# Moving six GEMM blocks of batch 0 into the attention of batch 1, with q,k transposed earlier and v loaded later

## Chip, cores and metric

The kernel runs on one core of a Trainium2 chip. The metric is the device time in microseconds (us) of one execution; before the change it is 345.62 us, the median of 3 runs (345.62 to 345.96).

Engines are named as in the profile: PE is TensorE's matmul, PEld its weight load, DVE is VectorE, ACT is ScalarE, POOL is GpSimd, SP is SyncE (which only issues transfers here). A name such as L375 is line 375 of the kernel.

## What is computed

Eight batches of an attention with forget gates, each with 8 heads, 576 positions and 64 elements a head, and after it a two-layer network with exact Gelu over the 4608 resulting rows.

```python
# attention: q, k, v are (8, 8, 576, 64) float32, f is (8, 8, 576)
scores = scale * np.matmul(q, k.transpose(0, 1, 3, 2))
cum = np.cumsum(np.log(np.clip(f, 0.0001, 1.0)), axis=-1)
decay = cum[:, :, :, None] - cum[:, :, None, :]
scores = np.where(causal, -1e9, scores + decay)
attn = softmax(scores)                 # max taken off, exp, divided by the sum
out = np.matmul(attn, v)
# network: w_in is (512, 2048), w_out (2048, 512)
x = out.transpose(0, 2, 1, 3).reshape(4608, 512)
h = x @ w_in
g = 0.5 * h * (1.0 + erf(h / sqrt(2)))
return g @ w_out
```

## The kernel before

All of it works in bfloat16 with float32 sums. Heads are taken in pairs (`i` = 0 to 3). For one pair the scores stand transposed, keys on partitions, in four tiles (`t` = 0 to 3); ACT takes the exp; POOL masks the diagonal blocks (in batch 0, and for the first pair of batch 1, PE adds the mask instead). The decay is not added to the scores: v is weighed with a factor for each key (`weigh_v`, on POOL), and a further column holds the weights themselves, so that the AV product gives sum and normalizer together. DVE normalizes, and PE transposes x again for the first GEMM.

The first GEMM of a batch is 16 blocks of 128 columns of w_in (`ffb` = 0 to 15), each four matmuls of 128x512 and a Gelu on ACT. The second GEMM of a batch is spread between the scores of the next batch's attention (`take(fill, n)` takes n of its matmuls). That can't be done with all of batch 0's second GEMM in batch 1, where only its first half for two row blocks (`gemm2_half(0, 0)`, 16 matmuls) is taken; the rest goes into batch 2.

PSUM has eight banks: two score tiles of two banks (`s`), two `o` banks and two `m` banks.

```python
s_psum = ctx.enter_context(tc.tile_pool(name="s_psum", bufs=2, space=PSUM))
o_psum = ctx.enter_context(tc.tile_pool(name="o_psum", bufs=2, space=PSUM))
m_psum = ctx.enter_context(tc.tile_pool(name="m_psum", bufs=2, space=PSUM))
...
v_sb = consts.tile([P, H, NBLK, D], FP32)          # one buffer for v of any batch
...
def transposes_first(b, i, which, pool, tag):      # q or k of a head pair, 12 transposes
    src = qk_of[b][which]
    ps = pool.tile([P, JT, PT], BF16, tag=tag, name="ps_f")
    ...
    op = nc.scalar.copy if b == i == which == 0 else nc.vector.tensor_copy
    op((qT, kT)[which][i]..., ps...)
...
def weigh_v(b, i, eng=nc.gpsimd):
    ...
    eng.tensor_tensor(vw_of[b][:, hs, :, 0:D], v_sb[:, hs, :, :], w..., Alu.mult)
    eng.tensor_copy(vw_of[b][:, hs, :, D], w)
...
def gemm1(c, ffb, kts=range(4), ps=None, act=True):
    src = xT(c) if c < B else tails
    if ps is None:
        ps = m_psum.tile([P, TC], FP32, tag="m", name="ps1")
    for kt in kts:
        nc.tensor.matmul(ps, w_in_sb[:, kt, ffb * P : (ffb + 1) * P], src[:, kt, 0:TC],
                         start=(kt == 0), stop=(kt == n_dm - 1))
    if n_dm - 1 in kts and act:
        gelu(c, ffb, ps)
    return ps
```

In the attention of batch 0 the loads for what follows are issued (q, k and w by POOL, v by SP):

```python
load_w_in(0)
weigh_v(0, 1)
load_w_in(1)
weigh_v(0, 2)
weigh_v(0, 3)
nc.gpsimd.memset(v_sb[:, :, 0, 0:1], 0.0)
load_v(1, 0, 4)
load_v(1, 4, 8)
load_w_in(2)
load_w_in(3)
load_qk_tokens(1, 0, 4)
load_qk_tokens(1, 4, 8)
```

The attention of batch 1, and the loop around it:

```python
FILL_1 = [[0, 0, 0, 0], [0, 0, 0, 0], [2, 2, 2, 2], [2, 2, 2, 2]]
...
def second_attention():
    b, fill = 1, gemm2_half(0, 0)
    ...
    nc.scalar.activation(warm[0:1, 0:1], warm[0:1, 0:1], Act.Exp)   # loads the exp table
    weigh_v(1, 2)
    weigh_v(1, 3)
    for i in range(HP):
        for t in range(4):
            scores(b, i, t)
            if i == 0 and t < 3:
                transposes(t + 1, *((m_psum, "m") if t == 1 else (o_psum, "o")))
            take(fill, FILL_1[i][t])
            if i and t in (1, 2):
                av(i - 1, t - 1)
            if i > 1 and t == 0:
                to_xT(b, i - 2, nc.vector.tensor_copy, o_psum, "o")
            if (i, t) == (1, 3):
                load_qk_tokens(2, which="k")
            if (i, t) == (3, 0):
                transpose_dma(2, 0, 4)
                transpose_dma(2, 4, 8)
    to_xT(b, HP - 2, nc.vector.tensor_copy, o_psum, "o")
    av(HP - 1, 0)
    av(HP - 1, 1)
    both = s_psum.tile([P, 2, 1024], BF16, tag="s", name="ps_x2")
    gemm1_begin(1, both)          # blocks 0 to 3 of the first GEMM, around the last x transposes
    x_tail(1)
    load_w_out(2)
    load_w_out(3)
    load_v(2)

for b in range(B):
    ...                            # the attention of batch b; batch 0 does blocks 0 to 3 too
    for ffb in range(0 if b > 1 else 4, n_ff):
        gemm1(b, ffb)
        if b == 0:
            if ffb == 14:
                for which in range(2):
                    transposes_first(1, 0, which, o_psum, "o")
            if ffb == 12:
                weigh_v(1, 0)
                load_w_out(0)
                load_w_out(1)
                weigh_v(1, 1)
                load_qk_tokens(2, which="q")
        elif b + 1 < B:
            first, gap = (5, 3) if b == 1 else (0, 4)
            at, late = divmod(ffb - first, gap)
            if late == 0:
                untangle(b + 1, at)        # DVE: q,k of the next batch in their order
            if late == gap - 2:
                weigh_v(b + 1, at)
            ...
```

Of the kernel before, what the change touches and what calls it, by code (L numbers as in the profile page):

```python
# [8 lines left out]
FP32 = mybir.dt.float32  # L9
BF16 = mybir.dt.bfloat16  # L10
Act = mybir.ActivationFunctionType
# [7 lines left out]
HP = 4  # L19
# [33 lines left out]
def kernel(  # L53
# [60 lines left out]
    def load_v(b, h0=0, h1=H):  # L114
        if b >= B:
            return
        for n in range(NBLK):
            p0 = D if n == NBLK - 1 else 0
            nc.sync.dma_start(
                v_sb[p0:P, h0:h1, n, :],  # L120
                v[b, h0:h1, K0[n] + p0 : K0[n] + P].rearrange("h p d -> p h d"),
            )
# [48 lines left out]
    def load_w_out(c):  # L171
        kt = slice(c * n_ff // 4, (c + 1) * n_ff // 4)
        nc.gpsimd.dma_start(w_out_sb[:, kt, :], w_out_r[:, kt, :])
# [5 lines left out]
    cum = consts.tile([BH, S], FP32)  # L179
    wk = f_sb  # L180
    warm = consts.tile([P, TC], BF16)
    nc.vector.memset(warm, 0.0)
    nc.vector.memset(ones, 1.0)
    nc.vector.memset(wT[0:D, 4, :], 0.0)
# [68 lines left out]
    def weigh_v(b, i, eng=nc.gpsimd):  # L253

        if b not in vw_of:
            vw_of[b] = v_pool.tile([P, H, NBLK, D + 1], BF16, tag="vw", name=f"vw{b}")
        hs = slice(2 * i, 2 * i + 2)
        bh = b * H + 2 * i
        w = wT[:, :, bh : bh + 2].rearrange("p n h -> p h n")
        eng.tensor_tensor(  # L260
            vw_of[b][:, hs, :, 0:D],
            v_sb[:, hs, :, :],
            w.unsqueeze(3).to_broadcast([P, 2, NBLK, D]),
            Alu.mult,
        )
        eng.tensor_copy(vw_of[b][:, hs, :, D], w)
# [79 lines left out]
    def to_xT(b, i, copy, pool=m_psum, tag="m", ps=None):  # L346
        if ps is None:
            shape = [P, 2, 1024] if pool is s_psum else [P, XC]
            ps = pool.tile(shape, BF16, tag=tag, name="ps_x")
            if pool is s_psum:  # L350
                ps = ps[:, 0, 0:XC]
        for m in range(NBLK):
            nc.tensor.transpose(  # L353
                ps[:, m * P : (m + 1) * P], x_of[b, i][:, m, :, :], ident_bf
            )
        copy(xT(b)[:, i, :], ps)  # L356
# [10 lines left out]

    g_of = {}

    def gemm1(c, ffb, kts=range(4), ps=None, act=True):  # L370
        src = xT(c) if c < B else tails
        if ps is None:
            ps = m_psum.tile([P, TC], FP32, tag="m", name="ps1")
        for kt in kts:
            nc.tensor.matmul(  # L375
                ps,
                w_in_sb[:, kt, ffb * P : (ffb + 1) * P],
                src[:, kt, 0:TC],
                start=(kt == 0),
                stop=(kt == n_dm - 1),  # L380
            )
        if n_dm - 1 in kts and act:
            gelu(c, ffb, ps)
        return ps

    def gelu(c, ffb, ps):
        if c not in g_of:
# [133 lines left out]
    def take(gen, n):  # L521
        for _ in range(n):
            if next(gen, "end") == "end":
                return


    def first_attention():


        def transposes(i, pool, tag):  # L530
            transposes_first(0, i, 0, pool, tag)
            transposes_first(0, i, 1, pool, tag)

        def attend_head(i, h):
            attend(0, i, h, (0, 1, 2, 3, 4))
            normalize(0, i, h)

        warm_up(11)
        transposes(0, o_psum, "o")
        nc.vector.tensor_copy(key_of[D:P], key_of[0:D])  # L540
        nc.vector.tensor_copy(after[D:P], after[0:D])
        warm_up(2)
        scores(0, 0, 0)
        scores(0, 0, 1)
        transposes(1, m_psum, "m")
        scores(0, 0, 2)
        psw = o_psum.tile([P, NBLK, BH], FP32, tag="o", name="psw")
        for n in range(NBLK):
            nc.tensor.transpose(
                psw[:, n, :], wk[:, K0[n] : K0[n] + P], ident_fp[:BH, :BH]  # L550
            )
        scores(0, 0, 3)
        nc.vector.tensor_copy(wT[:, 0:4, :], psw[:, 0:4, :])
        nc.vector.tensor_copy(wT[D:P, 4, :], psw[D:P, 4, :])
        scores(0, 1, 0)
        transposes(2, m_psum, "m")
        scores(0, 1, 1)
        scores(0, 1, 2)
        transposes(3, m_psum, "m")
        scores(0, 1, 3)  # L560
        weigh_v(0, 0, nc.vector)
        gate = x_pool.tile([P, 1], FP32, tag="gate", name="gate")
        nc.gpsimd.tensor_copy(gate[D:P], v_sb[D:P, 0, 4, 0:1])
        load_w_in(0)
        weigh_v(0, 1)
        load_w_in(1)
        weigh_v(0, 2)
        weigh_v(0, 3)
        nc.gpsimd.memset(v_sb[:, :, 0, 0:1], 0.0)
        load_v(1, 0, 4)  # L570
        load_v(1, 4, 8)
        load_w_in(2)
        load_w_in(3)
        load_qk_tokens(1, 0, 4)
        load_qk_tokens(1, 4, 8)
        scores(0, 2, 0)
        scores(0, 2, 1)
        scores(0, 2, 2)
        scores(0, 2, 3)
        attend_head(0, 0)  # L580
        scores(0, 3, 0)
        attend_head(0, 1)
        scores(0, 3, 1)
        attend_head(1, 0)
        scores(0, 3, 2)
        attend_head(1, 1)
        scores(0, 3, 3)
        to_xT(0, 0, nc.vector.tensor_copy)
        attend_head(2, 0)
        attend_head(2, 1)  # L590
        to_xT(0, 1, nc.scalar.copy)
        attend_head(3, 0)
        both = s_psum.tile([P, 2, 1024], BF16, tag="s", name="ps_x2")
        to_xT(0, 2, nc.scalar.copy, ps=both[:, 0, 0:XC])
        attend_head(3, 1)
        gemm1_begin(0, both)
# [19 lines left out]

    FILL = [[7, 6, 3, 3], [1, 3, 3, 2], [1, 3, 3, 3], [1, 3, 3, 3], [8]]
    FILL_2 = [[8, 8, 8, 8], [8, 8, 4, 4], [4, 4, 4, 4], [4, 4, 4, 4], [8]]
    FILL_1 = [[0, 0, 0, 0], [0, 0, 0, 0], [2, 2, 2, 2], [2, 2, 2, 2]]

    def attention(b):

# [33 lines left out]
    def second_attention():  # L656


        b, fill = 1, gemm2_half(0, 0)

        def av(i, h):
            attend(b, i, h, (0, 1, 2, 3, 4))
            normalize(b, i, h)

        def transposes(i, pool, tag):
            for which in range(2):
                transposes_first(b, i, which, pool, tag)


        nc.scalar.activation(warm[0:1, 0:1], warm[0:1, 0:1], Act.Exp)  # L670
        weigh_v(1, 2)
        weigh_v(1, 3)
        for i in range(HP):
            for t in range(4):
                scores(b, i, t)
                if i == 0 and t < 3:
                    transposes(t + 1, *((m_psum, "m") if t == 1 else (o_psum, "o")))
                take(fill, FILL_1[i][t])
                if i and t in (1, 2):
                    av(i - 1, t - 1)  # L680
                if i > 1 and t == 0:
                    to_xT(b, i - 2, nc.vector.tensor_copy, o_psum, "o")
                if (i, t) == (1, 3):
                    load_qk_tokens(2, which="k")
                if (i, t) == (3, 0):
                    transpose_dma(2, 0, 4)
                    transpose_dma(2, 4, 8)
        to_xT(b, HP - 2, nc.vector.tensor_copy, o_psum, "o")
        av(HP - 1, 0)
        av(HP - 1, 1)  # L690
        both = s_psum.tile([P, 2, 1024], BF16, tag="s", name="ps_x2")
        gemm1_begin(1, both)
# [7 lines that stand above are left out]
            first_attention()  # L700
        elif b == 1:
            second_attention()
        else:
            attention(b)
        if b == 0:
            x_tail(0)
        for ffb in range(0 if b > 1 else 4, n_ff):
            gemm1(b, ffb)
            if b == 0:
                if ffb == 14:  # L710
                    for which in range(2):
                        transposes_first(1, 0, which, o_psum, "o")
                if ffb == 12:
                    weigh_v(1, 0)
                    load_w_out(0)
                    load_w_out(1)
                    weigh_v(1, 1)
                    load_qk_tokens(2, which="q")
            elif b + 1 < B:
                first, gap = (5, 3) if b == 1 else (0, 4)  # L720
                at, late = divmod(ffb - first, gap)
                if late == 0:
                    untangle(b + 1, at)
                if late == gap - 2:
                    weigh_v(b + 1, at)
                if ffb == (9 if b == 1 else 14):
                    load_qk_tokens(b + 2)
# [34 lines left out]
```

The softmax here doesn't subtract the row's maximum and nothing guards it: scores larger than these inputs give would overflow.

## Time and profile before

| | |
|---|---|
| time, median of 3 runs | 345.62 us |
| span of the profiled execution | 343.4 us |
| TensorE clock granted | 0.999 |
| DMA packets, bytes, mean rate | 99924, 43.03 MB, 125 GB/s |
| ACT, all Gelus (L392) | 144 of 597 ns |
| ACT, all exps (L299) | 128 of 836 ns on average |
| POOL, one weighing of v for a head pair (L260) | 1278 ns |
| POOL, one mask (L301) | 383 ns on average |

The profile is of one execution, with times from the span's start. A chain is followed back from the last instruction: at each step to what released it. A line of the chain gives start, length, engine, the tile written and the line. A line of the timeline adds shapes, and in brackets the idle time before it and what ended that. In a row of windows each engine has its busy us in the stretch and in brackets the number of its instructions. Matmuls overlap, so that a matmul's listed duration is longer than what it adds.

### The profile page before, as it was taken

The numbers are of one execution on the slowest core, as the hardware profiler recorded it, in microseconds if no ns is written. First come the engines' busy times: TensorE is split into PE (matmuls) and PEld (weight loads), VectorE is DVE, ScalarE is ACT, GpSimd is POOL, SyncE is SP. The second block draws the span as 40 slices with busy tenths as digits, with TensorE's granted clock in tenths as the row PEclk, the third lists the DMA queues.
The fourth block names the chain that finished last, engine by engine and source line by source line (L and its number), as shares of the span: only waits on it lengthen the run. The fifth ranks groups of instructions, "written<-read, shape, count | busy, mean of one in ns | idle before, by whom it ended". The sixth has DMA issues, their size and how long they took to land.

```text
span 343.4 us, 7895 instructions
## 1 busy us (share of the span) xinstructions
PE 328.6 (96%) x3182; PEld 174.7 (51%) x3227; DVE 187.0 (54%) x424; ACT 212.3 (62%) x296; POOL 124.2 (36%) x256
## 2 busy tenths in 40 slices
PE   7799999999999999999999999999999999999995
PEld 3574555445554456545654565446544654444443
DVE  5660355933467935796479646974597542020011
ACT  5986786773644787368746874687468755504600
POOL 8390672228328034543445243714261430000000
PEclk9999999999999999999999999999999999999999
DMA  8999999989993999578945896499900230011013
GB/s 117 178 176 194 201 166 153 170 158 148 237 184 102 139 192 188 82 101 165 211 121 73 141 212 139 71 160 198 169 31 2 65 88 31 2 61 61 0 38 87
DMA packets 99924, 43.03 MB, mean 125 GB/s; under 512 B 78704, under 2 KB 95344, under 8 KB 99888
## 3 DMA queue, kind: packets, MB, share of 16 engines
q1 hardware_dynamic: 82592, 28.37, 41.4%
q0 software_dynamic: 16896, 13.63, 27.2%
q8 instruction: 25, 0.41, 0.5%
q10 hardware_dynamic: 400, 0.52, 0.4%
q14 instruction: 11, 0.09, 0.1%
HBM read 36.85 MB, written 9.44 MB: 135 GB/s over the span
## 4 chain that ended last, share of the span: by engine, by line
PE 89%; issue 2%; POOL 2%; DVE 2%; ACT 2%; DMA 2%; POOLq 0%; ACTq 0%; DVEq 0%
PE ps L375 36%; PE ps L466 25%; PE o L320 9%; PE ps L408 8%; PE s L289 7%; PE ps L501 2%; ACT e L299 2%; DMA k<-in_k_dram 2%; PE ps_x L353 1%; DVE x L334 1%; POOL q L107 1%; PE ps_f L206 1%; POOL k L107 1%; DVE r L333 0%; DVE xT L356 0%
## 5 line engine op out<-in xcount | busy, mean ns | idle before, releaser
L392 ACT ACTIVATE g<-ps 128x512 bf16<-128x512 f32 x144 | 85.3, 597 | 81.1 <-PE ps L375 81.1
L299 ACT ACTIVATE e<-s 128x896 bf16<-128x896 f32 (+2 forms) x128 | 101.2, 836 | 28.5 <-PE s L289 26.8
L375 PE MATMUL ps<-xT,w_in_sb 128*128 128x512 bf16 x497 | 111.4, 379 | 0.8
L466 PE MATMUL ps<-w_out_sb,g 64*128 64x512 bf16 (+1 forms) x731 | 103.0, 376 | 0.8 <-issue 0.8
L375 PEld LDWEIGHTS <-w_in_sb 128*128 128x128 bf16 x576 | 56.0, 98 | 67.5 <-issue 1.8
L301 POOL TENSOR_SCALAR_AFFINE_SELECT e<-e 128x256 bf16<-128x256 bf16 (+1 forms) x135 | 49.2, 383 | 98.9 <-ACT e L299 98.6
L466 PEld LDWEIGHTS <-g 64*128 64x128 bf16 (+1 forms) x756 | 41.5, 94 | 40.4 <-issue 11.9
L244 DVE COPY qT<-tq 64x288 bf16<-64x288 bf16 x96 | 48.7, 507 | 1.4
L289 PE MATMUL s<-qT,kT 64*128 64x320 bf16 (+4 forms) x384 | 45.8, 276 | 3.6 <-ACT e L299 2.7
L260 POOL TENSOR_TENSOR vw<-v_sb,wT 128x640 bf16<-128x640 f32 x31 | 39.6, 1278 | 23.5 <-DMA v_sb<-in_v_dram 23.3
L320 PE MATMUL o<-vw,e 128*128 128x65 bf16 x960 | 36.8, 194 | 3.5 <-issue 2.4
L474 DVE COPY ot<-ps 128x512 f32<-128x512 f32 x26 | 17.9, 689 | 37.1 <-PE ps L466 35.2
L320 PEld LDWEIGHTS <-e 128*128 128x128 bf16 x960 | 34.8, 98 | 5.3 <-PE ps_x L353 0.3
L244 DVE COPY kT<-tk 64x288 bf16<-64x288 bf16 x96 | 33.0, 343 | 1.6
L334 DVE TENSOR_TENSOR x<-o,r 128x320 bf16<-128x320 f32 x64 | 31.4, 491 | 2.4 <-DVE r L333 0.2
L417 DVE COPY ot<-ps 128x512 f32<-128x512 f32 (+2 forms) x9 | 5.7, 632 | 48.8 <-PE ps L408 31.9
L289 PEld LDWEIGHTS <-kT 64*128 64x128 bf16 x384 | 19.5, 94 | 23.2 <-issue 9.7
L408 PE MATMUL ps<-w_out_sb,g 128*128 128x512 bf16 (+2 forms) x142 | 27.9, 355 | 0.1
L333 DVE RECIPROCAL r<-o 128x5 f32<-128x5 f32 x64 | 12.1, 189 | 27.6 <-PE o L320 27.5
L408 PEld LDWEIGHTS <-g 128*128 128x128 bf16 x144 | 13.5, 98 | 14.5
L476 DVE TENSOR_TENSOR ot<-ot,ps 128x512 f32<-128x512 f32 x26 | 17.9, 687 | 1.5
L365 POOL COPY tails<-xT 128x256 bf16<-128x256 bf16 x8 | 3.2, 399 | 31.3 <-DVE xT L356 31.3
(64 smaller groups left out, 158.1 us busy)
## 6 DMA issues: line engine op xcount, KB each, us to landing
out_dram<-ot SPq DMA_DIRECT2D x32, 256.0 KB, 2.3
v_sb<-in_v_dram SPq DMA_DIRECT2D x24, 256.0 KB, 5.3
q<-in_q_dram POOLq DMA_DIRECT2D x6, 576.0 KB, 6.1
k<-in_k_dram POOLq DMA_DIRECT2D x6, 576.0 KB, 8.2
v_sb<-in_v_dram SPq DMA_DIRECT2D x22, 128.0 KB, 5.1
w_in_sb<-in_moe_w_in_dram POOLq DMA_DIRECT2D x4, 512.0 KB, 6.7
w_out_sb<-in_moe_w_out_dram POOLq DMA_DIRECT2D x4, 512.0 KB, 8.4
q<-in_q_dram POOLq DMA_DIRECT2D x4, 144.0 KB, 4.6
```

What stands on the lines that cost most here:

```text
L244: nc.vector.tensor_copy(rows[:, odd], src[odd * D : (odd + 1) * D, 2 * i + h].rearrange("d j p -> d p j"),)
L260: eng.tensor_tensor(vw_of[b][:, hs, :, 0:D], v_sb[:, hs, :, :], w.unsqueeze(3).to_broadcast([P, 2, NBLK, D]), Alu.mult,)
L289: nc.tensor.matmul(to, *ab, start=half < 0, stop=half == 1 or not masked)
L299: nc.scalar.activation(et[:, :, z:c], st[:, :, z:c], Act.Exp, scale=scale)
L301: nc.gpsimd.affine_select(out=et[:, :, c0 + z : c0 + P], in_=et[:, :, c0 + z : c0 + P], compare_op=Alu.is_ge, fill=0.0, base=z, pattern=[[ ...
L320: nc.tensor.matmul(o[:, m, :], e_of[b, i, t][:, h, c : c + P], vw_of[b][:, 2 * i + h, n, :], start=(n == 0), stop=(n == m),)
L334: nc.vector.tensor_tensor(x_of[b, i][:, :, h, :], o[:, :, 0:D], r.unsqueeze(2).to_broadcast([P, NBLK, D]), Alu.mult,)
L375: nc.tensor.matmul(ps, w_in_sb[:, kt, ffb * P : (ffb + 1) * P], src[:, kt, 0:TC], start=(kt == 0), stop=(kt == n_dm - 1),)
L392: nc.scalar.activation(g_of[c][ffb], ps, Act.Gelu)
L408: nc.tensor.matmul(pss[ts][:, c0:c1], g_of[c][kt][:, ts * P : (ts + 1) * P], w_out_sb[:, kt, c0:c1], start=(kt == 0), stop=(kt == n_ff - 1),)
L466: nc.tensor.matmul(banks[r], g_of[c][kt][rows, ts * P : (ts + 1) * P], w_out_sb[rows, kt, :], start=kt == (steps.index("r") if r else 0), ...
L474: nc.vector.tensor_copy(ot, banks[1])
```

## The change

Six of the sixteen blocks (10 to 15) of batch 0's first GEMM are taken out of their place ahead of batch 1's attention and are computed between its scores. Their result is copied by DVE to SBUF (`h`), and their Gelu is taken later, in batch 1's first GEMM, so that ACT need not change its table between exps. That GEMM's odd blocks take an `o` bank, so that it has four banks.

Along with that: q and k of batch 1 are transposed a pair ahead, the first pair between blocks 8 and 9; scores are issued two at a time; AV products follow from the fifth group of scores on; v of batch 1 is loaded after w_in has landed (a small POOL copy waits for that), not beside the q and k loads; w_out, the weighing of v and the q,k loads of batch 2 are issued later. The purpose is that PE has other work where it waited for DVE's copies and ACT's exps, and that what is needed first is loaded first.

```diff
@@ -179,6 +179,8 @@
     warm = consts.tile([P, TC], BF16)
+    put_off = range(10, 16)
+    h_of = {n: consts.tile([P, TC], FP32, name=f"h{n}") for n in put_off}
@@ -367,10 +369,10 @@
-    def gemm1(c, ffb, kts=range(4), ps=None, act=True):
+    def gemm1(c, ffb, kts=range(4), ps=None, act=True, pool=m_psum, tag="m"):
         src = xT(c) if c < B else tails
         if ps is None:
-            ps = m_psum.tile([P, TC], FP32, tag="m", name="ps1")
+            ps = pool.tile([P, TC], FP32, tag=tag, name="ps1")
@@ -382,6 +384,16 @@
+    def gemm1_late(c):
+
+        for ffb in put_off:
+            ps = m_psum.tile([P, TC], FP32, tag="m", name="ps1")
+            for kt in range(n_dm):
+                gemm1(c, ffb, (kt,), ps, False)
+                if kt == n_dm - 1:
+                    nc.vector.tensor_copy(h_of[ffb], ps)
+                yield
@@ -566,9 +578,6 @@
         weigh_v(0, 3)
-        nc.gpsimd.memset(v_sb[:, :, 0, 0:1], 0.0)
-        load_v(1, 0, 4)
-        load_v(1, 4, 8)
         load_w_in(2)
@@ -616,7 +625,6 @@
-    FILL_1 = [[0, 0, 0, 0], [0, 0, 0, 0], [2, 2, 2, 2], [2, 2, 2, 2]]
@@ -666,26 +674,38 @@
+        transposes(1, m_psum, "m")
         nc.scalar.activation(warm[0:1, 0:1], warm[0:1, 0:1], Act.Exp)
-        weigh_v(1, 2)
-        weigh_v(1, 3)
-        ... (the loop over i and t above)
-        to_xT(b, HP - 2, nc.vector.tensor_copy, o_psum, "o")
+        wide = gemm1_late(0)
+
+        def x_first(i):
+            to_xT(b, i, nc.vector.tensor_copy, o_psum, "o")
+
+        between = [
+            lambda: take(wide, 8),
+            lambda: take(wide, 6),
+            lambda: (transposes(2, o_psum, "o"), take(wide, 2)),
+            lambda: (transposes(3, o_psum, "o"), take(wide, 4)),
+            lambda: (av(0, 0), av(0, 1), take(wide, 4)),
+            lambda: (av(1, 0), av(1, 1), x_first(0), take(fill, 2)),
+            lambda: (x_first(1), take(fill, 6)),
+            lambda: (av(2, 0), av(2, 1), take(fill, 8), x_first(2)),
+        ]
+        for n, work in enumerate(between):
+            i, t = divmod(2 * n, 4)
+            scores(b, i, t)
+            scores(b, i, t + 1)
+            work()
+            if n == 3:
+                weigh_v(1, 1)
+                load_qk_tokens(2, which="q")
+            if n == 5:
+                weigh_v(1, 2)
+                load_qk_tokens(2, which="k")
+            if n == 6:
+                weigh_v(1, 3)
+                transpose_dma(2, 0, 4)
+                transpose_dma(2, 4, 8)
         av(HP - 1, 0)
         av(HP - 1, 1)
@@ -704,18 +724,26 @@
-        for ffb in range(0 if b > 1 else 4, n_ff):
-            gemm1(b, ffb)
+        if b == 0:
+            gate = x_pool.tile([P, 1], FP32, tag="gate", name="gate")
+            nc.gpsimd.tensor_copy(gate, w_in_sb[:, 0, d_ff - 1 : d_ff])
+            nc.gpsimd.memset(v_sb[:, :, 0, 0:1], 0.0)
+            load_v(1)
+            nc.gpsimd.tensor_copy(gate, v_sb[:, 0, 2, 0:1])
+            load_w_out(0)
+            weigh_v(1, 0)
+            load_w_out(1)
+        for ffb in range(0 if b > 1 else 4, n_ff if b else put_off.start):
+            if b == 1 and ffb % 2:
+                gemm1(b, ffb, pool=o_psum, tag="o")
+            else:
+                gemm1(b, ffb)
+            if b == 1 and ffb % 2 == 0:
+                n = put_off[ffb // 2 - 2]
+                gelu(0, n, h_of[n])
             if b == 0:
-                if ffb == 14: ... if ffb == 12: ... (as above)
+                if ffb >= put_off.start - 2:
+                    transposes_first(1, 0, ffb - put_off.start + 2, o_psum, "o")
```

More of the change, by code (lines that the diff above doesn't have):

```diff
@@ L667, in transposes @@
                 transposes_first(b, i, which, pool, tag)
+        transposes(1, m_psum, "m")
         nc.scalar.activation(warm[0:1, 0:1], warm[0:1, 0:1], Act.Exp)
-        weigh_v(1, 2)
-        weigh_v(1, 3)
[L673 to L687, printed above, removed]
-        to_xT(b, HP - 2, nc.vector.tensor_copy, o_psum, "o")
+        wide = gemm1_late(0)
[26 more added lines that the diff above has]
+                transpose_dma(2, 4, 8)
         av(HP - 1, 0)
@@ L706 @@
             x_tail(0)
-        for ffb in range(0 if b > 1 else 4, n_ff):
-            gemm1(b, ffb)
-            if b == 0:
[L710 to L718, printed above, removed]
+        if b == 0:
[15 more added lines that the diff above has]
+                gelu(0, n, h_of[n])
+            if b == 0:
+                if ffb >= put_off.start - 2:
+                    transposes_first(1, 0, ffb - put_off.start + 2, o_psum, "o")
             elif b + 1 < B:
```

## The prediction, made before the changed kernel was run

> **What bounds the kernel now.** I read the page first: share of busy time, then the chain that ended last. Then I cut the stretch of batch 1's attention out of the chain, and asked the windows what each engine did in it.
>
> ```profile
> PE 328.6 (96%) x3182; PEld 174.7 (51%) x3227; DVE 187.0 (54%) x424; ACT 212.3 (62%) x296; POOL 124.2 (36%) x256
> PE 89%; issue 2%; POOL 2%; DVE 2%; ACT 2%; DMA 2%; POOLq 0%; ACTq 0%; DVEq 0%
> ```
>
> TensorE (PE) is the bound: 89% of the chain is PE work. The change adds no PE work and removes none, so it can only win back holes. Where are they? The windows, for the first GEMM of batch 0 (its last part), the attention of batch 1, and the first GEMM of batch 1:
>
> ```profile
> 33.90:37.90 4.00, 3.95 (x20) 1.69 (x20) 0.00 (x0) 2.70 (x5) 1.11 (x1) 1.00 1.28 191
> 37.90:59.53 21.63, 19.74 (x324) 12.46 (x328) 12.96 (x28) 16.99 (x22) 13.20 (x27) 1.00 1.17 175
> 59.53:72.60 13.07, 13.02 (x61) 5.75 (x62) 11.10 (x33) 8.63 (x15) 2.03 (x3) 1.00 1.03 180
> ```
>
> After the length of the stretch come PE, PEld, DVE, ACT, POOL, then clock, DMA share and GB/s. The two GEMMs leave PE no hole; the attention between them leaves 1.9 us. The chain inside it shows whose they are:
>
> ```profile
> 37.90 0.50 PE ps_f L206 x14
> ...
> 38.42 0.76 DVE qT L213
> 39.18 0.68 DVE kT L213
> ...
> 41.76 0.80 ACT e L299
> ...
> 44.23 0.31 ACT e L299
> 44.54 0.29 issue
> 44.83 0.55 ACT e L299
> 45.38 0.25 issue
> 45.62 0.63 ACT e L299
> ```
>
> The transposed q and k are copied out by VectorE (0.76 + 0.68 us) before the first score can start, and only one GEMM block lies beside that. Then, up to 47.3, there is no filler, and PE goes at the pace of ScalarE's exps.
>
> Busy time hides part of the hole, so I add up the PE work from 37.90 to 59.53 by its chain pieces. Four pairs of q,k transposes at 0.74: 2.96. One GEMM block, 4 matmuls at 0.218: 0.87. Scores: 0.54+0.32+0.45+0.35 for the first head pair, three times about 1.07 (0.27+0.24+0.29+0.27) for the others: 4.87. AV: 8 x 0.47 = 3.76. Filler: 16 at 0.27 (pieces of 0.54 for two) = 4.32. Four x transposes at 0.45: 1.80. The next GEMM's first block: 0.87. Sum 19.45 of 21.63: **2.2 us of holes** is all there is to win here.
>
> The loads are the other limit. POOL waited 10 us for v:
>
> ```profile
> 36.79 1.28 POOL L260 TENSOR_TENSOR vw<-v_sb,wT 128x640 bf16<-128x640 f32 x1 [10.02 <-DMA v_sb<-in_v_dram]
> 42.23 1.28 POOL L260 TENSOR_TENSOR vw<-v_sb,wT 128x640 bf16<-128x640 f32 x1 [0.30 <-DMA v_sb<-in_v_dram]
> ```
>
> So v's halves landed at about 36.8 and 42.2, and DMA moved about 192 GB/s from 25 to 44, saturated. The issues of batch 1's q and k, by issue time plus time to landing: q heads 0-3 22.9+11.5 = 34.4, k heads 0-3 36.4, q heads 4-7 38.5, k heads 4-7 40.6; the last quarter of w_in 22.2+10.1 = 32.3.
>
> **What the skill says.** (1) The Trainium skill, "Perfetto Trace Analysis", Identifying the Most-Contended Engine: matmul busy share is no good measure for TensorE, because of pipelining. The trace agrees: a 128x512 matmul is listed at 379 ns while 41 of them take 8.95 us, 218 each; hence the sum above. (2) "TensorE: Matmul & The Clock Gate", Back-to-back issue gap: about N/2.4 + 2.5 ns, 216 for 512 columns. It agrees with 218; that section's 131 ns for a sustained stream isn't seen. (3) "ScalarE: Activation LUTs", What ACT_TABLE_LOAD costs: 1283 ns plus a drain of 1380 ns. The trace has the 1.28 us (at 40.26), but the next activation starts at 41.55, so no such drain. (4) "DMA: Bandwidth & Descriptors", Issuing engines are not separate DMA queues: all issues share 16 engines and interleave. It agrees: v issued at 23.4 by SyncE needed 13.2 us beside the q, k and w_in loads.
>
> **The change part by part.** Let T be the end of block 9, now the last of the shortened GEMM. Block 14 ended at 37.90 before; take off blocks 10-14 (20 x 0.218 = 4.36) and put in the 12 q transposes (0.37) that now precede block 9: T = 33.9.
>
> Removed: 24 matmuls, 5.2 us, from the first GEMM. Added: the same 24, between score pairs, so no PE time is saved. Also added: six VectorE copies to h, 128x512 f32 from PSUM, 0.69 us each as such copies are listed (0.689): 4.1 us. VectorE had 12.96 us busy in 21.63; 17 in about 24 fits. The six late Gelus (0.60 us each) go into the GEMM of batch 1. Per two blocks, 1.74 us of PE, ScalarE then has three; three in a row took 1.57 there. It keeps up, barely, and odd blocks now take o banks, so four banks cushion it.
>
> Walking the new order from T, PE: k transposes +0.37, next pair's q and k to +1.1 (its k bank waits for block 9's Gelu, +0.65 to +0.74). VectorE has the first k copied at +1.15, so the old wait of 1.44 us is covered except 0.05. Two scores to +1.85, 8 late matmuls to +3.6. ScalarE: Gelu to +0.65, table to +1.95, exps at +2.15 to +3.75. Scores to +4.2, 6 matmuls +5.6, scores +6.2, transposes +6.95, 2 matmuls +7.4, scores +8.0, transposes +8.8, 4 matmuls +9.7, scores +10.2, AV of the first pair (its bank waits for the last k copy, +10.2) +11.2, 4 matmuls +12.1, scores +12.7, AV +13.65, wait 0.3 for the bank of the x transposes (VectorE's scaling), +14.4, filler 2 +14.9, scores +15.5, x +15.95, filler 6 +17.3, scores +17.9, AV +18.9, filler 8 +20.7, x +21.2, last AV +22.2, first GEMM matmuls +23.1, last x +23.55. In this walk each pair of exps (1.5 to 1.7 us) has about 3 us of PE work beside it, so ScalarE no longer sets the pace. I priced late matmuls and filler at 0.218; a chunk of two cost the old filler 0.54 instead of 0.436, so for the eight chunks I add 0.1 each: +24.35. That is 58.25, against 59.53: **1.3 us won**.
>
> v: it now starts after w_in has landed. Without v beside it, w_in's last quarter (32.3 before) should land near 30.7, q heads 0-3 near 32.2, k heads 0-3 near 33.8. They are needed at T-1.24 = 32.7 and T = 33.9: just in time. The bytes ahead of v's end are those of before less a bit of w_out (0.15 MB, 0.8 us), so v ends near 41 to 42. GpSimd then needs 1.37 us for the first weighing (36.79 to the next instruction at 38.15): 42.8, against AV at T+10.2 = 44.1. Behind it on GpSimd stand a w_out issue (0.79), 15 masks (the timeline has the first three of a head pair in 1.01 us and the other two in 0.77: 5.3), three weighings (4.1) and two q,k issues (0.84 and 0.82): 11.9 us, ending at 54.7; the last AV wants it at T+21.2+0.8 = 55.9. About 1 us of slack in both.
>
> Sum: 345.62 - 1.3 = **344.3 us**.
>
> **Rivals.** *GpSimd and v become the bound.* v's end plus 13.3 us is GpSimd's last mask, so each us of v beyond 42.6 delays the last AV one for one; the chain of before already has 0.41 us of a mask (to 57.1) just ahead of it. With v at 43.9 the gain is gone; at 46, the time is 347.7. For it: v starts 9 us later. Against: the DMA engines move the same bytes and are saturated anyway. *q and k come late.* If w_in and q,k run no faster without v, the first scores wait for k until 36.4 instead of 33.9, and 2.5 us go: 346.8. Against: v's bytes shared those engines from 23.4 on. *ScalarE becomes the bound in batch 1's GEMM*: at 0.60 per Gelu without overlap, three are 1.80 against 1.74; over six pairs 0.4 us: 344.7. *No holes are left at all* (DMA kind, fewer switches): 2.2 us won, 343.4.
>
> **Range and chances.** The best case is bounded by the holes, 343.4, with some error of the sum: 343.0. The bad ones reach 346.8 and 347.7; each I take for one in ten, and to go half that far more often than all of it: 346.1. 2% is 6.9 us, three times the holes; faster by that is next to impossible, slower needs v late by over 8 us.
>
> **What would show it.** Right: PE busy nearly without gaps in the attention; the copies of q,k no longer in the chain ahead of the first score; exps no longer in the chain; the first GEMM of batch 1 starting near 58.1. Wrong: an AV or a mask waiting for the weighed v, LDWEIGHTS of q or k waiting for DMA near 34, matmuls of batch 1's GEMM waiting for Gelus, or the gain lost later, in batch 2's attention, whose q and k are loaded some us later than before.

## The result, and the profile after

The changed kernel takes 349.84 us (median of 4 runs, 348.80 to 351.91) against 345.62: a ratio of 1.0128, 95% interval 1.0091 to 1.0165. It is slower by 4 us where 1.3 us of gain was predicted. The profiled execution is one of its longer ones (350.69 us), so that the two traces differ by 5.3 us.

The page after, engines and chain:

```profile
PE 330.2 (95%) x3180; PEld 174.7 (50%) x3227; DVE 190.6 (55%) x430; ACT 211.1 (61%) x296; POOL 124.8 (36%) x258
PE 78%; POOL 7%; DMA 5%; SPq 4%; issue 2%; DVE 1%; ACT 1%; POOLq 0%; DVEq 0%
```

PE was 89% of the chain and is 78% now; GpSimd, DMA and the issuing of SyncE (SPq) have taken its place. But this happens after the place of the change. PE's timeline of the changed kernel, from batch 1's first GEMM on (start, length, line, shapes, count, and in brackets the idle time before it and what ended that):

```profile
58.23 13.11 PE L377 MATMUL ps<-xT,w_in_sb 128*128 128x512 bf16 x59
71.28 0.37 PE L291 MATMUL s<-qT,kT 64*128 64x256 bf16 x4
...
83.00 0.38 PE L478 MATMUL ps<-w_out_sb,g 128*128 128x512 bf16 x1 [0.16 <-issue]
86.54 0.24 PE L322 MATMUL o<-vw,e 128*128 128x65 bf16 x2 [3.16 <-POOL e L303]
87.50 1.74 PE L322 MATMUL o<-vw,e 128*128 128x65 bf16 x28 [0.73 <-POOL e L303]
```

The same rows of the kernel before:

```profile
59.36 13.21 PE L375 MATMUL ps<-xT,w_in_sb 128*128 128x512 bf16 x59
72.50 0.37 PE L289 MATMUL s<-qT,kT 64*128 64x256 bf16 x4
...
84.44 1.11 PE L320 MATMUL o<-vw,e 128*128 128x65 bf16 x30
```

Up to the first score of batch 2 the changed kernel is ahead by 1.22 us (71.28 against 72.50): the gain was there. Then, at the first AV of batch 2, PE waits 3.16 + 0.73 us for a mask on GpSimd. The windows add what follows (PE first after the length, the granted clock third from the end):

```profile
83.00:88.00 5.00, 1.02 (x10) 0.40 (x10) 1.26 (x2) 0.00 (x0) 4.99 (x11) 1.00 1.08 151
88.00:92.00 4.00, 4.00 (x43) 2.25 (x43) 1.37 (x4) 1.12 (x2) 1.18 (x4) 0.57 1.28 232
```

GpSimd has no free moment (busy for 4.99 of 5.00 us), PE is busy for 1.02, and in the 4 us after that TensorE is granted 0.57 of its clock: another 4.00 x 0.43 = 1.7 us lost. What made the mask late is in the chain (start, length, engine, line):

```profile
51.60 7.60 DMA k<-in_k_dram
...
59.22 1.28 SPq L232
...
60.55 1.85 SPq L232
...
62.44 7.32 SPq L232
...
69.85 0.53 SPq L119
...
73.23 5.52 DMA v_sb<-in_v_dram
...
78.97 1.28 POOL vw L262
...
86.15 1.67 POOL e L303 x5
```

Read downwards: batch 2's k is issued at 51.6 (before: 48.3) and lands at 59.2. SyncE works in order, so the transposing transfers (L232), which need k, wait for it; the last of them takes 7.3 us to issue; only then comes v of batch 2 (L119), which lands at 79 instead of 75.2. SyncE before:

```profile
54.86 1.29 SPq L230 DMA_TRANSPOSE tk<-k  x1
...
57.83 2.73 SPq L230 DMA_TRANSPOSE tk<-k  x1
60.65 11.17 SPq L119 DMA_DIRECT2D v_sb<-in_v_dram  x5
```

There the queue was held up as well, only on v's own transfers (11.17 us) instead of on the last k. From the start of that last transfer to the end of v's issue it is 13.99 us before and 11.82 after. So the long issue is not what is new; the start is, as k came at 54.86 and now comes at 59.22.

GpSimd works in order too: four weighings and two load issues, then the masks. GpSimd before, at the same place:

```profile
75.18 1.28 POOL L260 TENSOR_TENSOR vw<-v_sb,wT 128x640 bf16<-128x640 f32 x1 [13.03 <-DMA v_sb<-in_v_dram]
...
82.29 2.68 POOL L301 TENSOR_SCALAR_AFFINE_SELECT e<-e 128x256 bf16<-128x256 bf16 x8
```

82.29 - 75.18 is 7.11 us without a pause; after it is 86.08 - 78.97 = 7.11. v's delay of 3.79 us went through to the masks in full. And before, there was little slack to use up: a head pair has five masks, which take 1.7 us (the last line of the chain), so that they ended near 84.0, and PE took them from 84.44 on: by this estimate, half a us of slack. Against it stand the delay of 3.79 us and a PE that comes 1.22 us earlier.

### The profile page after: what moved, and what is told of

Read it like the earlier page. It is cut to its first block, busy times and chain, and to the rows that moved or that the text cites. A ratio compares the mean times of both kernels' runs of the same rounds, so it can differ in the third digit from the quotient of the medians.

```text
span 348.7 us, 7904 instructions
## 1 busy us (share of the span) xinstructions
PE 330.2 (95%) x3180; PEld 174.7 (50%) x3227; DVE 190.6 (55%) x430; ACT 211.1 (61%) x296; POOL 124.8 (36%) x258
## 4 chain that ended last, share of the span: by engine, by line
PE 78%; POOL 7%; DMA 5%; SPq 4%; issue 2%; DVE 1%; ACT 1%; POOLq 0%; DVEq 0%
PE ps L377 31%; PE ps L478 23%; PE o L322 8%; PE ps L420 8%; PE s L291 6%; DMA k<-in_k_dram 4%; SPq L232 3%; POOL vw L262 3%; DMA v_sb<-in_v_dram 2%; POOL e L303 1%; POOL q L107 1%; SPq L119 1%; PE ps_x L355 1%; POOL k L107 1%; PE ps_f L208 1%
## 5 line engine op out<-in xcount | busy, mean ns | idle before, releaser
L404 ACT ACTIVATE g<-ps 128x512 bf16<-128x512 f32 x138 | 81.7, 597 | 76.8 <-PE ps L377 76.2
L377 PE MATMUL ps<-tails,w_in_sb 128*128 128x512 bf16 x63 | 14.3, 378 | 0.1
```

The costliest lines, as they stand in the source:

```text
L404: nc.scalar.activation(g_of[c][ffb], ps, Act.Gelu)
```

## Experiments

**Theory A**: moving batch 2's k load behind a weighing delays k, the transposing transfers, v, weighings and masks, in this order, and a wait and a lowered clock follow. **Rival B**: the GEMM of batch 1 with the late Gelus and borrowed banks, or something later, costs it.

The first kernel loads k with q:

```diff
             if n == 3:
                 weigh_v(1, 1)
-                load_qk_tokens(2, which="q")
+                load_qk_tokens(2)
             if n == 5:
                 weigh_v(1, 2)
-                load_qk_tokens(2, which="k")
```

> The changed kernel, with the load of batch 2's k issued together with that of q (some 3 us earlier) instead of after the next weighing. Theory A (k of batch 2 lands late; the transposing transfers and then v of batch 2 stand behind it on SyncE; GpSimd weighs v late, its masks come late, PE waits): v of batch 2 lands near 75.5 instead of 78.9, PE's wait ahead of the first AV of batch 2 shrinks from 4 us to below 1, time 344.5 to 346. Rival B (the late Gelus and the four banks in batch 1's GEMM, or the lowered TensorE clock, are the cause): time stays at 349 to 350.

347.40 us, ratio 1.0052 (1.0034 to 1.0070): 2.4 us better than the changed kernel. v landed at 76.4, 2.5 us earlier, and the wait fell to 1.16 + 0.73:

```profile
84.02 0.24 PE L322 MATMUL o<-vw,e 128*128 128x65 bf16 x2 [1.16 <-POOL e L303]
84.98 1.49 PE L322 MATMUL o<-vw,e 128*128 128x65 bf16 x28 [0.73 <-POOL e L303]
```

Better than B allows, worse than A expected. k is issued at 48.0, as before the change, but lands at 56.4 instead of 54.9, with q issued just ahead of it (47.2; before, 41.1). And PE starts batch 2 at 70.76, 1.74 us ahead of the kernel before. With half a us of slack, by the estimate above, it would wait for the masks even if v were not late at all; no run shows that by itself. TensorE's clock was lowered again, to 0.50 from 86 to 88 and 0.66 to 90: 1.7 us.

The second moves `load_v(2)` from behind the loads of w_out to just ahead of `transpose_dma(2, ...)`, so that SyncE issues v first.

> The changed kernel, with v of batch 2 issued on SyncE ahead of the transposing transfers of q and k instead of behind them; k as late as in the changed kernel. Theory A: v is issued near 55 and lands before 68, GpSimd no longer waits for it, PE's 4 us wait goes, time 344 to 345.5. Theory A', that the late q and k themselves hold PE up: the wait stays, now at the scores of batch 2, and the time stays above 348. Rival B: 349 to 350.

354.98 us, ratio 1.0265 (1.0224 to 1.0306), worse than the change itself. v landed at 71.3 (A expected 68) and the AV no longer waited, but the wait moved to the scores, as A' has it. SyncE, and PE at the scores of batch 2:

```profile
61.70 8.55 SPq L232 DMA_TRANSPOSE tq<-q  x1
```

```profile
78.82 0.39 PE L291 MATMUL s<-qT,kT 64*128 64x256 bf16 x1 [8.04 <-DVE kT L246]
```

Now the transposing transfers stand behind v, and PE waits 8 us for kT. So k isn't just in v's way; both are needed at about the same time, and swapping them in the queue only chose which is late.

The third puts `nc.gpsimd.tensor_copy(gate[0:D], tq_of[2][1][0:D, H - 1, 0, 0:1])` ahead of `load_w_out(2)`, so that w_out waits for the transposed k.

> The changed kernel, with the second half of w_out loaded only after the last transposed k of batch 2 has landed (a small GpSimd copy waits for it). If the 7.3 us issue of the last transposing transfer came from w_out's traffic beside it, that issue falls to 2 us and v of batch 2 lands by 75; the wait then moves to the second GEMM of batch 0, whose weights come later, so the time says little (346 to 351). If the late k alone is to blame, the issue stays near 7 us.

```profile
60.08 1.64 SPq L232 DMA_TRANSPOSE tk<-k  x1
```

The issue fell from 7.32 to 1.64 us, and with v's issues it took 6.3 us instead of 11.8. So w_out's two transfers, issued at 59.3 in the changed kernel, hold SyncE's queue up; which transfer bears it depends on which is next. This isn't what makes v late, though: v landed at 75.4, 18.9 us after k (56.6). In all twelve profiled executions in which v stands behind the transposing transfers, from the kernel before to the last one below, GpSimd starts on v 18.8 to 20.6 us after the first transposing transfer of k, which waits for k (54.4 to 59.4). So v comes late by about as much as k does. No AV waited for a mask here, but PE came to it only at 86.96, having waited 2.5 us for w_out, as expected. There is one run, 348.31 us.

The fourth takes the kernel before and makes k late, alone:

```diff
-                if (i, t) == (1, 3):
+                if (i, t) == (2, 3):
                     load_qk_tokens(2, which="k")
```

> The kernel before, with one thing alone: k of batch 2 loaded one head pair later (some 4 us). Theory A: v of batch 2 lands later by some 3 us, GpSimd's masks and the first AV of batch 2 by as much, time 348 to 350. Rival B, where that load doesn't matter: 345.6.

349.55 us, ratio 1.0120 (1.0093 to 1.0147), as A has it and as large as the change's own net loss, with nothing else of the change in it. In the profiled execution, the shortest of four (348.10 us), k landed at 58.9 and v at 78.4, and PE waited for the mask:

```profile
85.96 0.24 PE L320 MATMUL o<-vw,e 128*128 128x65 bf16 x2 [1.06 <-POOL e L301]
```

The next four test the other end: GpSimd's masks no longer stand behind all the weighings. Only the first weighing stays in batch 1's GEMM:

```diff
-                if late == gap - 2:
+                if late == gap - 2 and (b > 1 or at == 0):
                     weigh_v(b + 1, at)
-                if ffb == (9 if b == 1 else 14):
+                if b > 1 and ffb == 14:
                     load_qk_tokens(b + 2)
 ... in attention(b):
-                if t == 1 and i == 0:
+                if b == 2 and (i, t) == (0, 3):
+                    weigh_v(2, 1)
+                    load_qk_tokens(3)
+                    weigh_v(2, 2)
+                    weigh_v(2, 3)
+                    load_v(3)
+                if b > 2 and t == 1 and i == 0:
                     load_v(b + 1)
```

> The changed kernel; only GpSimd's order in batch 2 is changed: of the four weighings of v, three, and the q,k load issues of batch 3, stand behind the masks of the first head pair instead of ahead of them (and the load of v of batch 3 behind them). k of batch 2 and v land as late as in the changed kernel (79). Theory A: the first masks are ready near 82.5 instead of 88, the PE wait and the lowered clock go, and the 1.2 us won in batch 1's attention stay: 344 to 345. Rival (batch 1's GEMM with late Gelus, or something later, loses the time): above 348.

> As the run with the masks first, and batch 2's k is loaded with its q too. Theory A: there is then slack of some 3 us, and the time is the same as with the masks first alone or 0.3 us less: 343.8 to 344.8.

> The kernel before, with GpSimd's order in batch 2 changed in the same way. Before, v landed just in time for the masks (PE had no wait there), so theory A expects nothing to be won: 345.3 to 345.9. If the order is worth something by itself, the time falls by 0.5 us or more.

346.69 us, ratio 1.0036 (1.0017 to 1.0054), with k early 346.37 and 1.0026 (1.0003 to 1.0050), and in the kernel before 347.35 and 1.0050 (1.0030 to 1.0069). All three expectations missed by over 1 us, all in the same direction. The wait at the first AV was gone in each. (In the first of them v landed at 75.5, not at 79 as expected; with the old order its masks would have begun near 82.6, and PE asked for them at 82.5.) But the edit had a cost of its own, ahead of batch 2's GEMM; PE of the first of the three:

```profile
106.44 13.84 PE L377 MATMUL ps<-xT,w_in_sb 128*128 128x512 bf16 x62 [2.54 <-DMA xT<-x]
```

The GEMM waited 2.54 us for x (1.66 in the kernel before with this edit, 1.60 with k early). v of batch 3 goes into the buffer that the last weighing of batch 2's v leaves free. That weighing now comes after the masks, so in the kernel before with this edit v of batch 3 is issued from 85.7 on instead of 82.2, and batch 2's last x transfer, which stands behind it on SyncE in both, at 104.8 instead of 101.3. It is the same fault on a smaller scale: a load was moved, and what stands behind it in the queue was not followed up.

The eighth is the first of these with v of batch 1 loaded where it was before the change (`load_v(1, 0, 4)` and `load_v(1, 4, 8)` ahead of `load_w_in(2)`, no gates, and the first weighing ahead of both w_out loads).

> As the run with the masks first, but v of batch 1 is loaded as before the change, ahead of the last w_in quarters and of q and k. The prediction's rival, that q and k then come late for the earlier transposes: PE waits for them near 34 for some 2 us, the GEMM of batch 1 starts near 60 instead of 58.2, time 345.5 to 347. If loading v last is worth nothing: 344 to 345.

348.61 us, ratio 1.0070 (1.0040 to 1.0100), 1.6 us above the expected range. PE near block 9:

```profile
34.26 0.56 PE L208 MATMUL ps_f<-ident_bf,q 96*64 96x96 bf16 x12 [1.49 <-DMA q<-in_q_dram]
...
36.27 0.47 PE L208 MATMUL ps_f<-ident_bf,k 96*64 96x96 bf16 x10 [0.48 <-DMA k<-in_k_dram]
```

PE waits 2.0 us for q and k, and batch 2's attention starts at 73.4 instead of 71.4. Loading v last is worth these 2 us; without it the change gains nothing in batch 1 (73.2 before).

The last three change SyncE's order as well: `load_v(3)` moves behind the first `x_dma` of batch 2, `transpose_dma(3, ...)` behind the second.

```diff
                     weigh_v(2, 3)
-                    load_v(3)
 ...
                         x_dma(b, i - 1)
+                    if b == 2 and i == 1:
+                        load_v(3)
-                if b == 2 and t == 1 and i == 1:
+                if b == 2 and t == 1 and i == 2:
                     transpose_dma(3, 0, 4)
```

> As the run with the masks first, and SyncE's order in batch 2 mended: v of batch 3 is issued behind the first transposing transfer of x, and q and k of batch 3 are transposed behind the second one, so that the last x of batch 2 doesn't wait on SyncE. Theory A (two queues in order, GpSimd's and SyncE's, are all that took the gain): no wait of 2.5 us ahead of batch 2's first GEMM, the 1.2 us of batch 1 stay: ratio 0.995 to 0.998, 344 to 345. Rival (something else in the changed kernel costs it): ratio 1.0 or more.

> As that, with k of batch 2 loaded with its q. Theory A: the same ratio within 0.001, as v's landing no longer decides.

> The kernel before with both orders mended in the same way. Theory A: nothing to win without the change, ratio 0.999 to 1.001; the loss of the run of before with the masks first alone, 0.5%, goes, as it was SyncE's order. If the orders by themselves are worth it, the ratio is as low as with the change.

With the change: 344.40 us, ratio 0.9964 (0.9942 to 0.9985), as A has it. With k early too: 344.05, **0.9943** (0.9922 to 0.9963), faster than both kernels. That is 0.0021 lower where A expected at most 0.001, but the intervals of the two overlap. In the kernel before: 345.50, 0.9986 (0.9974 to 0.9998), a little better than A's range. So of 0.57% the orders alone bring 0.14, and the change with k early 0.43, some 1.5 us. With k left late the change brings 0.22, and the intervals of those two overlap. In the fastest, the first AV finds its masks done; GpSimd and PE:

```profile
76.33 1.28 POOL L262 TENSOR_TENSOR vw<-v_sb,wT 128x640 bf16<-128x640 f32 x1 [15.94 <-DMA v_sb<-in_v_dram]
...
77.71 1.73 POOL L303 TENSOR_SCALAR_AFFINE_SELECT e<-e 128x256 bf16<-128x256 bf16 x5
```

```profile
82.59 1.11 PE L322 MATMUL o<-vw,e 128*128 128x65 bf16 x30
```

v is no earlier than in the first experiment (76.4), but the masks end at 79.4, and PE asks for them at 82.6. With k left late, v lands at 78.7, and the AV at 84.9 doesn't wait either; in the old order the masks would begin 7.11 us after v, at 85.8.

Stage lengths sum it up. ScalarE loads a table at the start of each attention and of each GEMM; the times between these loads, in us (the profiled executions):

| | batch 2's attention starts | its length | its GEMM's length | span |
|---|---|---|---|---|
| before | 73.22 | 25.05 | 21.86 | 343.4 |
| changed | 72.14 | 30.97 | 22.01 | 348.7 |
| k early | 71.62 | 29.01 | 22.01 | 346.7 |
| before, k late | 73.52 | 27.44 | 21.87 | 346.0 |
| masks first | 71.39 | 24.90 | 24.70 | 344.6 |
| before, masks first | 73.10 | 25.04 | 23.68 | 345.2 |
| both orders, k early | 71.51 | 24.91 | 22.01 | 342.0 |

The changed kernel's loss is 30.97 - 25.05 = 5.92 us in one stage: 3.89 of waiting, 1.7 of clock, 0.3 left over. It also comes out of the causes, as an estimate: v later by 3.79, PE earlier by 1.22, less 0.5 of slack, and 1.7 of clock make 6.2. B falls: the GEMM of batch 1 lasts no longer (13.11 against 13.21 us for the same 59 matmuls), and the later stages take as long as before, to within half a us in all.

## Why the prediction was wrong

What it said of batch 1's attention held nearly. 1.3 us was to be won, and 1.22 was, up to batch 2's first score. That the figures agree so well is in part luck: T, the end of block 9, was 34.4 instead of 33.9 (waits of 0.5 us for q and 0.4 for k), and the walk from there to the GEMM took less than was counted. The AV of the second head pair waited 0.61 us for a weighed v, a sign of being wrong that had been named. q heads 0-3 landed at 32.8 (32.2 predicted). GpSimd's last mask ended at 55.55 (54.7 predicted); the last AV came at 55.75. ScalarE kept up with three Gelus in two blocks (1.73 us a round, from 0.62 for a late Gelu on), so that rival fell.

The step that failed is the sum itself: "Sum: 345.62 - 1.3". It ended at 58.25, with all that follows taken as unchanged, and merely earlier. The paragraph ahead of it counted "two q,k issues (0.84 and 0.82)" on GpSimd as time that GpSimd spends, and did not ask where that puts the data that they load. The last part did name "the gain lost later, in batch 2's attention, whose q and k are loaded some us later than before", but nothing was worked out for it: neither that k's issue moves from 48.3 to 51.6, nor that v of batch 2 stands behind k's transposing transfers on SyncE, nor that GpSimd before ran without a pause from v's landing to masks that PE took some half a us later. The missing term was +5.9 us. Part of it is the gain itself: a PE that comes 1.22 us earlier waits so much longer when the masks don't come earlier with it. The words "slower needs v late by over 8 us" looked at v of batch 1 only; v of batch 2, late by 3.79 us, cost 5.9.

The first rival had the right mechanism ("GpSimd and v become the bound"), one batch too early. The second, late q and k, is what loading v last avoids: 2.0 us measured without that, where 2.5 was said.

The clock was not in the prediction. The Trainium skill, "TensorE: Matmul & The Clock Gate", Part 1: The HAM clock gate, says that an idle window of some 3.4 us halves TensorE's clock until a busy one has passed. The changed kernel comes close to that (3.16 + 0.73 us of waiting, then 0.57 for 4 us). But the kernel with k early got 0.50 after waits of only 1.16 + 0.73 us with 0.24 us of work between them, and the kernel before with k late got 1.00 after 1.06 + 0.73. Nor is it always 1.00 in that kernel: its four executions took 348.10, 349.07, 350.04 and 350.87 us at mean clocks of 0.999, 0.998, 0.994 and 0.989. The page has the window run freely, which would make it a matter of where the wait falls; this fits these numbers, but no run here shows it.

## What to carry to other kernels

A sum over the stage that is changed is not enough where engines and queues work in order: follow each moved load to the instruction that first needs it, through every queue that it stands in, and ask of the profile before how much slack that instruction had. Where one engine works without a pause until another takes its result (7.11 us here), there is little slack (half a us here), for a load that comes later or for a consumer that comes earlier. Where two loads are both just in time, swapping them made it worse here (354.98 us); taking other work out from ahead of the consumer helped (344.05).

## What was not expected of the hardware

A queue that works in order was held up by transfers that another engine had issued. The last transposing transfer and v's loads behind it took SyncE 11.6 to 14.0 us to issue in eleven kernels in which GpSimd issued w_out's two loads near that time, and 6.3 us in the one run where these were held back. Which transfer bears it varies: the transposing one took 7.3 us in the changed kernel, 2.8 in the kernel before with k late, and 1.6 with w_out held back.

Waits of nearly the same length on PE had very different costs: 1.8 us lengthened batch 2's attention by 2.4 us in one profiled execution (k late, clock 1.00), and 1.9 us by 4.0 in another (k early, clock 0.50 and then 0.66).
